# Attention and a SoLU feed-forward on one core: row 0's softmax chain, the scaling of x and the block sums one product later, squares and weight combinations at other places

## The chip, the cores and the metric

The kernel runs on one core of a Trainium2 chip. The metric is the device time of one execution in microseconds (us). Engines are named as in the profile: PE is TensorE's matmul queue (PEld its weight loads), DVE is VectorE, ACT ScalarE, POOL GpSimd, SP the engine whose queue issues most of the DMAs. Each engine works through its own queue in the order in which the kernel was written; between engines there are only waits on semaphores.

## The reference

```python
q_n, k_n = rmsnorm(q, g_q), rmsnorm(k, g_k)              # (8, 12, 448, 64)
scores = q_n @ k_n^T / sqrt(64)
attn = exp(scores - max) / (sum + 1e-9)
x = (attn @ v) with the heads put side by side           # (3584, 768)
h = x @ w_in                                             # (3584, 1024)
sm = exp(h - max) / (sum + 1e-9)
solu = h * sm
ln = (solu - mean) / sqrt(var + 1e-6) * g_ln
out = ln @ w_out                                         # (3584, 768)
```

All of it is float32 in the kernel; the weights arrive as float64 and are converted on the core.

## The kernel before, in words

`fast_path` has three stages, written one after the other in one order for all engines (`manual_schedule`): what stands earlier in the code stands earlier in its engine's queue. `unit(f)` does a piece of TensorE work and then whatever is due; `later(n, f)` makes f due at the end of the n-th unit from there (of the running one for n = 1); `follow(parts, i, f)` puts f right behind part i. Things due at the same unit's end go by their due time and then in the order in which they were entered.

**Attention** (to about 308 us). The 96 heads are worked in 24 quads, m = 0 to 23, two pairs of heads each. A quad m has seven blocks of scores (`score(0)` to `score(6)`, L876), each followed on ACT by an exponential (L836; the last one's output is El), and seven of values (`value`, L888). The sums over keys are made by TensorE from additions of the exponentials (es, L896 and L902 on DVE), for two quads at a time behind every even quad (L948). Beside them, for quads ahead, runs the norm of q and k: `squares` (ACT, L687), `row_sums` (DVE, L693), `fold_sums` (POOL, L703 and L704), `rsqrt_seed` (ACT, a logarithm and an exponential, L710 and L711), `rsqrt_step` (DVE), `normalise` (POOL, L726), `qk_transpose` (DVE, L747) and `gains` (ACT, L742). From quad 6 on (`early`) the squares are made one quad sooner. The conversion of w_in (`convert_w`, quads 5 to 21) and its combinations for the fast product (`combine_in`, POOL, L567) are spread over the quads.

**The w_in products** (about 308 to 568 us). x is worked in 14 groups g of 256 rows, as 2 x 2 blocks with seven products instead of eight (six matmul records each, all on L1097). The order of the parts around group g is

p6(g), p5(g), p7(g), p1(g+1), p4(g), p2(g+1), p3(g).

p6 and p7 add to bank A what p1 left in it, and ACT copies the bank between (L1104: q1 after p1, u2 after p6, u3 after p7). p5 and p3 share bank B, p4 has bank D; both lie in one tile, BD. DVE adds bank and copy into h and takes the running maximum (`plus`, L1113): row 1 of a group is complete after p4, row 0 after p3. Then each row of 128 goes through the chain of `done`: exponential (ACT, L1168), product with h (DVE, L1182), deviations (ACT, L1193), spread (POOL, L1198 to L1201, its last output is `shift`), norm (ACT, L1221), transpose and store (DVE, L1231). In groups 0 to 11 the chain has these six steps (`two_pass`), in the last two groups another form.

Beside it the next group's operand is made: `scale` multiplies x by the inverse sums in three pieces (DVE, L1045; pieces 0 and 1 the two halves of the first 128 rows, piece 2 the other 128 rows), `sizes` takes its squares for a check of range (ACT, L1056, into the tile of the block sums), `block_sums` makes s1 and s2 (POOL, L1073, L1074; they wait for `sizes`), then s3 and s4 (L1076, L1077). p1 needs piece 0, p2 piece 1, p6 needs s2, p5 s1, p7 s3, p3 s4. Behind every third part of groups 0 to 6 a piece of w_out is converted (ACT L538, L539; DVE L545, L546; ACT L551), and 44 combinations of w_out (POOL, L567) stand behind the parts from number 30 on, from part 54 on behind each.

**The w_out products** (from 568 us) follow in the same way with prepared operands.

Of the kernel before, what the change touches and what calls it, by code (L numbers as in the profile page):

```python
# [366 lines left out]
def fast_path(  # L367
# [628 lines left out]
    gs = {}  # L996
# [82 lines left out]
    def products(g, done):  # L1079


        k = {}
        n = DFF // 2

        def mul(bank, a, i, begin=True):
            a11, a12, a21, a22 = gs[g, "A"]
            sm = gs[g, "s"]
            a = {"a11": a11, "a12": a12, "s3": a21, "a22": a22, "s1": sm[:, 0], "s2": sm[:, 1], "s4": sm[:, 2]}[a]
            if begin:
                if bank in "AC" or bank == "B" and g == NG - 1:  # L1090
                    k[bank] = ps_t.tile([P, 512], FP32, tag="t", name=bank, bufs=3)[:, 0:n]
                else:
                    if "BD" not in k:
                        k["BD"] = ps_t.tile([P, 2, 512], FP32, tag="o", name="BD", bufs=1)
                    k[bank] = k["BD"][:, "BD".index(bank), 0:n]
            for c in range(HD):
                nc.tensor.matmul(  # L1097
                    k[bank], a[:, c], w_in[i][:, c],
                    start=begin and c == 0, stop=c == HD - 1, skip_group_check=not begin,
                )  # L1100

        def part(name, bank):
            k[name] = sums_in.tile([P, 512], FP32, tag="part", name=name, bufs=4)[:, 0:n]
            nc.scalar.copy(k[name], k[bank])  # L1104

        def plus(row, col, bank, x):
            t = 2 * g + row
            d = mt.setdefault(t, {})  # L1110
            out = half_of(t, col)
            top = small.tile([P, 1], FP32, tag="top", name="top")
            nc.vector.tensor_tensor_reduce(  # L1113
                out, k[bank], k[x], 1.0, d.get("top", -3.4e38), OP.add, OP.max, top
            )
            d["top"] = top

        def p1():
            mul("A", "a11", 0)
            part("q1", "A")  # L1120

        def p2():
            mul("C", "a12", 1)
            plus(0, 0, "C", "q1")

        def p6():
            mul("A", "s2", 5, False)
            part("u2", "A")

        def p5():  # L1130
            mul("B", "s1", 3)

        def p7():
            mul("A", "s3", 4, False)
            part("u3", "A")
            plus(1, 1, "B", "u3")

        def p4():
            mul("D", "a22", 6)
            plus(1, 0, "D", "u3")  # L1140
            done(1)

        def p3():
            mul("B", "s4", 2, False)
            plus(0, 1, "B", "u2")
            done(0)

        return {1: p1, 2: p2, 3: p3, 4: p4, 5: p5, 6: p6, 7: p7}
# [90 lines left out]
    def in_parts():  # L1239
        def done(g, i):  # L1240
            t = 2 * g + i
            ff_max(t)
            waits = {
                (NG - 2, 1): (1, 2, 3, 5, 5), (NG - 2, 0): (1, 2, 4, 6.25, 7),
                (NG - 1, 1): (1, 2, 3.25, 6.75, 7.25), (NG - 1, 0): (2.25, 4.25, 6.75, 8, 8.75),
            }.get((g, i))
            if two_pass(t):
                steps = (ff_exp, ff_mult, ff_deviations, ff_spread_of, ff_norm, ff_spread)
                waits = (1, 2, 3, 4, 5, 7 if i else 8)
            else:  # L1250
                steps = (ff_exp, ff_mult, ff_moments, ff_norm, ff_spread)
            for x, f in zip(waits, steps):
                later(x, lambda f=f: f(t))

        p = [products(g, lambda i, g=g: done(g, i)) for g in range(NG)]
        parts = [p[0][1], p[0][2]]
        for g in range(NG):
            turn = [p[g][6], p[g][5], p[g][7], p[g][4], p[g][3]]
            x = len(parts)
            if g + 1 < NG:  # L1260
                turn[3:] = [p[g + 1][1], p[g][4], p[g + 1][2], p[g][3]]
            parts += turn
            if g + 1 < NG:
                follow(parts, x, lambda g=g: scale(g + 1, 0))
                follow(parts, x + 1, lambda g=g: scale(g + 1, 1))
                follow(parts, x + 2, lambda g=g: scale(g + 1, 2))
                if g + 2 < NG:
                    follow(parts, x + 3, lambda g=g: load_r(g + 2))
                follow(parts, x + 2, lambda g=g: sizes(g + 1))
                follow(parts, x + 3, lambda g=g: block_sums(g + 1, 0))  # L1270
                follow(parts, x + 4, lambda g=g: block_sums(g + 1, 1))
            if g + 2 < NG:
                follow(parts, x + 4, lambda g=g: load_x(g + 2))
        return parts
# [171 lines left out]
    def follow(p, i, f):  # L1446
        g = p[i]

        def both():
            g()  # L1450
            later(1, f)

        p[i] = both
# [22 lines left out]
    EARLY = 6  # L1476
    steps_at = (5, 6, 8, 9, 11, 12, 14, 15, 17, 18, 20, 21)
    combines_at = {10 + x + 2 * (x // 4): (x,) for x in range(8)}
    combines_at.update({22: (8, 9), 23: (10, 11)})
    inverts_at = {4: (0,), 8: (1,), 10: (2,), 14: (3,), 16: (4,), 20: (5,), 22: (6,)}  # L1480
    wq += [(moe_w_out, c + k, i) for c in range(HF) for k in (0, HF) for i in range(2)]
    again = [(w, w.shape[0] // P, i) for w in (moe_w_in, moe_w_out) for i in range(-(-w.shape[0] // P * w.shape[1] // S))]
# [30 lines left out]
    with tc.manual_schedule():  # L1513
# [68 lines left out]
        for m in range(1, NQ):  # L1582
            a, b = 2 * m, 2 * m + 1
            next1 = m + 1 < NQ
# [4 lines left out]
            def score(x):  # L1589
                unit(lambda: both_scores(m, x))  # L1590
# [50 lines left out]
            else:  # L1641
                if next1:
                    rsqrt_step(norms[m + 1])
                    if m == 2:
                        add_pair(1, 3, 4)
                        quads[1]["terms"].append((2, quads[1]["E", 5]))
                    normalise(a + 2)
                    normalise(b + 2)
                if early:
# [7 lines left out]
                if m == NQ - 1:  # L1657
                    scale(0)
                score(0)
                if m > 3 and not early:  # L1660
                    squares(a + 4)
                    row_sums(a + 4)
                score(1)
                if next1:
                    qk_transpose(a + 2)
                if m > 3 and not early:
                    squares(b + 4)
                    row_sums(b + 4)
                if m <= 3:
                    score(2)  # L1670
                    squares(a + 4)
                    row_sums(a + 4)
                if next1:
                    qk_transpose(b + 2)
                if m > 3:
                    score(2)
                score(3)
                if m <= 3:
                    squares(b + 4)
                    row_sums(b + 4)  # L1680
                if next2:
                    fold_sums(m + 2)
                for x in combines_at.get(m, ()):
# [7 lines left out]
                score(5)  # L1691
                if m in steps_at:
                    low_bits[1]()
                if next1:
                    gains(m + 1)
                add_pair(m, 0, 1)
                add_to(m, 0, 2, nc.vector)
# [4 lines left out]
                    add_pair(m, 3, 4)  # L1702
                value(2)
                score(6)
                if m in steps_at:
                    join()
                if next2:
# [218 lines left out]
```

## Time and profile before

| what | us |
|---|---|
| median of 3 runs (804.02 to 805.27) | 804.84 |
| the profiled execution | 802.92 |
| its span, first to last instruction | 801.1 |
| PE busy | 784.1 |
| DVE busy | 596.2 |
| ACT busy | 502.0 |
| POOL busy | 499.0 |

The mean granted TensorE clock of the profiled execution is 0.998. In the timeline a row has its start and its length in us, the engine (with a q where its queue issues a DMA), the source line, the operation, output<-inputs by the program's names, the shapes and the number of merged instructions; in brackets how long the engine was idle before it and what ended that.

### The profile page before, as it was taken

What the parts mean: (1) busy time and instruction counts of PE and PEld (TensorE: products, weight loads), DVE (VectorE), ACT (ScalarE), POOL (GpSimd) and SP (SyncE); (2) the same over time, 40 slices, a digit from 0 to 9 for tenths busy, and PEclk for the clock granted to TensorE, in tenths of its full rate; (3) what the DMA queues carried; (4) which work ended last, traced back from release to release, by engine and by line L of the source; (5) the groups of instructions that cost most, each with busy time, mean ns of one, the idle gap of its engine ahead of it and who ended that gap; (6) DMA issues with size and microseconds to landing.
All of it is one profiled execution on the core that took longest, in us unless ns stands there. A gap on an engine that the chain in (4) does not pass through costs nothing.

```text
span 801.1 us, 15270 instructions
## 1 busy us (share of the span) xinstructions
PE 784.1 (98%) x5374; PEld 479.2 (60%) x5374; DVE 596.2 (74%) x1061; ACT 502.0 (63%) x822; POOL 499.0 (62%) x618
## 2 busy tenths in 40 slices
PE   8999999999999999999999999999999999999996
PEld 4444444444444444444444444444799999999996
DVE  6877988999899873667776666676896785876854
ACT  6776988788988853677767656554515445464510
POOL 2555453664465461444657589898787777867861
PEclk9999999999999999999999999999999999999999
DMA  9889988888988256566767767673657557357212
GB/s 179 173 167 186 207 196 177 178 201 178 178 193 186 68 152 143 139 171 171 199 162 183 161 151 182 163 177 74 204 151 236 170 178 265 127 197 252 84 61 84
DMA packets 279851, 134.28 MB, mean 168 GB/s; under 512 B 190356, under 2 KB 264916, under 8 KB 279764
## 3 DMA queue, kind: packets, MB, share of 16 engines
q1 hardware_dynamic: 265924, 123.31, 61.7%
q10 hardware_dynamic: 13840, 9.90, 4.6%
q8 instruction: 44, 0.72, 0.4%
q14 instruction: 43, 0.35, 0.1%
HBM read 96.12 MB, written 37.04 MB: 166 GB/s over the span
## 4 chain that ended last, share of the span: by engine, by line
PE 63%; DVE 9%; POOL 8%; DMA 6%; ACT 5%; SPq 4%; issue 4%; DVEq 0%; ACTq 0%; POOLq 0%
PE A L1352 14%; PE s L876 13%; PE o L888 13%; PE B L1352 7%; PE sm L948 4%; PE A L1097 4%; PE BD L1097 4%; PE C L1352 3%; POOL w_out L567 3%; SPq L644 2%; PE C L1097 2%; DMA xg<-xd 1%; DMA raw<-in_moe_w_out_dram 1%; POOL xsum L1077 1%; DVE ub L1231 1%
## 5 line engine op out<-in xcount | busy, mean ns | idle before, releaser
L726 POOL TENSOR_TENSOR qkn<-qk,ny 128x896 f32<-128x896 f32 x45 | 77.2, 1736 | 103.3 <-DVE ny L720 89.3
L876 PE MATMUL s<-qkT 64*64 64x448 f32 x1288 | 139.9, 542 | 0.3 <-ACT qkT L742 0.2
L836 ACT ACTIVATE E<-s 128x896 f32<-128x896 f32 x144 | 124.4, 920 | 18.8 <-PE s L876 18.0
L888 PE MATMUL o<-E,v 64*64 64x448 f32 x1104 | 120.2, 536 | 0.0
L876 PEld LDWEIGHTS s<-qkT 64*64 64x64 f32 x1288 | 65.3, 191 | 60.8 <-issue 41.6
L1352 PE MATMUL A<-w_out,sums 128*128 128x192 f32 x392 | 80.0, 327 | 1.1 <-DVE u L1366 1.1
L1352 PE MATMUL B<-w_out,sums 128*128 128x192 f32 x392 | 79.9, 327 | 0.4 <-DVE P L1414 0.4
L888 PEld LDWEIGHTS o<-E,v 64*64 64x64 f32 x1104 | 42.0, 133 | 56.5 <-issue 49.9
L1097 PE MATMUL A<-w_in,xg 128*128 128x512 f32 x168 | 74.9, 594 | 0.5 <-ACT u L1104 0.5
L1097 PE MATMUL BD<-w_in,xsum 128*128 128x512 f32 x156 | 71.5, 594 | 1.6 <-DVE top L1113 1.5
L1352 PEld LDWEIGHTS A<-w_out,sums 128*128 128x128 f32 x392 | 66.1, 190 | 2.1 <-issue 1.4
L1352 PEld LDWEIGHTS B<-w_out,sums 128*128 128x128 f32 x392 | 66.3, 190 | 1.0 <-DVE P L1414 0.9
L747 DVE STREAM_TRANSPOSE qkT<-qkn 128x896 f32<-128x896 f32 x46 | 50.9, 1106 | 13.6 <-POOL qkn L726 13.5
L1097 PEld LDWEIGHTS A<-w_in,xg 128*128 128x128 f32 x168 | 31.7, 190 | 41.2 <-issue 38.2
L896 DVE TENSOR_TENSOR es<-E 128x896 f32<-128x896 f32 x46 | 55.5, 1206 | 0.5 <-ACT E L836 0.4
L693 DVE TENSOR_REDUCE part<-sq 128x28 f32<-128x896 f32 x46 | 48.0, 1074 | 7.7 <-ACT sq L687 7.7
L1097 PEld LDWEIGHTS BD<-w_in,xsum 128*128 128x128 f32 x156 | 29.3, 190 | 40.2 <-issue 35.8
L567 POOL TENSOR_TENSOR w_out<-w_out 128x384 f32<-128x384 f32 x44 | 50.2, 1142 | 1.7
L1221 ACT ACTIVATE u<-u,shift,he 128x1024 f32<-128x1024 f32 x28 | 34.7, 1239 | 26.2 <-POOL shift L1201 18.0
L1073 POOL TENSOR_TENSOR xsum<-xg 128x384 f32<-128x384 f32 x14 | 14.0, 1000 | 52.1 <-ACT xsum L1056 41.1
L1352 PE MATMUL A<-w_out,s 128*128 128x192 f32 x224 | 45.6, 326 | 0.0
L1182 DVE CUSTOM_DVE_ANT_0 u<-h,u 128x1024 f32<-128x1024 f32 x24 | 36.1, 1503 | 7.7 <-ACT u L1168 7.3
(180 smaller groups left out, 1672.2 us busy)
## 6 DMA issues: line engine op xcount, KB each, us to landing
ur<-ud SPq DMA_DIRECT2D x60, 256.0 KB
ud<-ub SPq DMA_DIRECT2D x112, 128.0 KB
xd<-xo SPq DMA_DIRECT2D x48, 224.0 KB
qk<-in_q_dram SPq DMA_DIRECT2D x92, 112.0 KB
qk<-in_k_dram SPq DMA_DIRECT2D x92, 112.0 KB
v<-in_v_dram SPq DMA_DIRECT2D x23, 448.0 KB
out_dram<-P SPq DMA_DIRECT2D x19, 384.0 KB
raw<-in_moe_w_in_dram SPq DMA_DIRECT2D x12, 512.0 KB
```

The source lines that it names most:

```text
L567: nc.gpsimd.tensor_tensor(o, p, q, OP.subtract)
L693: nc.vector.tensor_reduce(norms[m]["part"][:, i], st[n]["sq"], AX, OP.add)
L726: e.tensor_tensor(d["qkn"].rearrange("p (s b) d -> p s b d", s=2), d["qk"].rearrange("p s (b d) -> p s b d", d=32), y.rearrange("p (s b) - ...
L747: nc.vector.transpose(d["qkT"].rearrange("p s t -> p (s t)"), d["qkn"].rearrange("p b d -> p (b d)"))
L836: nc.scalar.activation(e, s[:, :, 0:S], AF.Exp)
L876: nc.tensor.matmul(s[i * D : (i + 1) * D, h, 0:S], qkT[hh, i, 1, keys], qkT[hh, i, 0], start=True, stop=True)
L888: nc.tensor.matmul(d["o"][h * D : (h + 1) * D, i, 0:S], d["v"][pp, h, kc], d["E", kc][pp, h], start=kc == 0, stop=kc == NK - 1,)
L896: nc.vector.tensor_tensor(e, d["E", x], d["E", y], OP.add)
L1097: nc.tensor.matmul(k[bank], a[:, c], w_in[i][:, c], start=begin and c == 0, stop=c == HD - 1, skip_group_check=not begin,)
L1182: nc.vector.tensor_tensor_reduce(u, h, u, 1.0, 0.0, OP.mult, OP.add, total)
L1221: nc.scalar.activation(d["u"], d["u"], AF.Identity, scale=d["e"], bias=d["shift"])
L1352: nc.tensor.matmul(k[bank], a[:, c].rearrange("p a i -> p (a i)"), w_out[:, area, i, c], start=begin and c == 0, stop=c == KC - 1, skip_gr ...
```

## The change

It touches three things.

- w_in products, row 0 of each two-pass group: every step of its chain but the last comes one unit later. Row 1 is untouched. Scaling: pieces 1 and 2 both come behind part x+2 (p7), not behind x+1 and x+2; `sizes` and both `block_sums` come one part later. Since p1 of a group may now be written before the tile of its block sums exists, `mul` looks that tile up only where a product uses it.
- Attention, quads 2 to 5 in the code's m: for m = 3 the squares and row sums of quad 5 stand behind `score(0)` and `score(1)`, where m = 4 and later have them; for m = 2 both squares come before the second `qk_transpose`; for m = 2 to 5 `gains` stands behind `score(6)` rather than behind `score(5)`.
- Combinations of w_in: numbers 8 and 9 stand ahead of the normalisation in quad 22; 10 and 11 take their former place there, and quad 23 has none.

```diff
         def mul(bank, a, i, begin=True):
             a11, a12, a21, a22 = gs[g, "A"]
-            sm = gs[g, "s"]
-            a = {"a11": a11, "a12": a12, "s3": a21, "a22": a22, "s1": sm[:, 0], "s2": sm[:, 1], "s4": sm[:, 2]}[a]
+            if a in ("s1", "s2", "s4"):
+                a = gs[g, "s"][:, ("s1", "s2", "s4").index(a)]
+            else:
+                a = {"a11": a11, "a12": a12, "s3": a21, "a22": a22}[a]
...
                 steps = (ff_exp, ff_mult, ff_deviations, ff_spread_of, ff_norm, ff_spread)
-                waits = (1, 2, 3, 4, 5, 7 if i else 8)
+                waits = (1, 2, 3, 4, 5, 7) if i else (2, 3, 4, 5, 6, 8)
...
                 follow(parts, x, lambda g=g: scale(g + 1, 0))
-                follow(parts, x + 1, lambda g=g: scale(g + 1, 1))
-                follow(parts, x + 2, lambda g=g: scale(g + 1, 2))
+                follow(parts, x + 2, lambda g=g: (scale(g + 1, 1), scale(g + 1, 2)))
...
-                follow(parts, x + 2, lambda g=g: sizes(g + 1))
-                follow(parts, x + 3, lambda g=g: block_sums(g + 1, 0))
-                follow(parts, x + 4, lambda g=g: block_sums(g + 1, 1))
+                follow(parts, x + 3, lambda g=g: sizes(g + 1))
+                follow(parts, x + 4, lambda g=g: block_sums(g + 1, 0))
+                follow(parts, x + 5, lambda g=g: block_sums(g + 1, 1))
...
-    combines_at.update({22: (8, 9), 23: (10, 11)})
+    combines_first = {22: (8, 9)}
+    combines_at[22] = (10, 11)
...
+                    for x in combines_first.get(m, ()):
+                        combine_in(x)
                     normalise(a + 2)
                     normalise(b + 2)
...
-                if m > 3 and not early:
+                if m > 2 and not early:
                     squares(a + 4)
                     row_sums(a + 4)
                 score(1)
                 if next1:
                     qk_transpose(a + 2)
-                if m > 3 and not early:
+                if m > 2 and not early:
                     squares(b + 4)
                     row_sums(b + 4)
-                if m <= 3:
+                if m == 2:
                     score(2)
                     squares(a + 4)
                     row_sums(a + 4)
-                if next1:
-                    qk_transpose(b + 2)
-                if m > 3:
-                    score(2)
-                score(3)
-                if m <= 3:
+                    score(3)
                     squares(b + 4)
                     row_sums(b + 4)
+                    qk_transpose(b + 2)
+                else:
+                    if next1:
+                        qk_transpose(b + 2)
+                    score(2)
+                    score(3)
...
-                if next1:
+                if next1 and early:
                     gains(m + 1)
...
                 score(6)
+                if next1 and not early:
+                    gains(m + 1)
```

## The prediction

> **What bounds the kernel now.** I read the page's head first, then TensorE's waits between 308 and 568 us (the w_in products; line, releaser, us in all, times, longest).
>
> ```profile
> span 801.1 us, 15270 instructions
> PE 784.1 (98%) x5374; PEld 479.2 (60%) x5374; DVE 596.2 (74%) x1061; ACT 502.0 (63%) x822; POOL 499.0 (62%) x618
> ```
> ```profile
> ...
> PE A L1097 <- ACT u L1104: 0.5, 1, 0.5
> ```
>
> TensorE runs without a break but for short waits, and the change leaves its work alone. So the whole question is how many waits go and how many come. An idle time here is less than what it costs, since TensorE also restarts slowly; I therefore take losses from stretches of time. Next view: stretches from the start of one group of w_in products (or one quad of heads) to the start of the next (start:end, length, then busy time of PE, PEld, DVE, ACT, POOL, clock, DMA).
>
> ```profile
> 331.09:554.85 223.76, 219.50 (x506) 94.65 (x505) 150.74 (x280) 148.78 (x248) 159.03 (x211) 1.00 0.65 162
> 367.60:386.81 19.21, 18.56 (x43) 7.81 (x42) 13.76 (x26) 13.98 (x25) 10.08 (x16) 1.00 0.76 189
> 386.81:406.08 19.27, 18.70 (x44) 7.73 (x43) 15.20 (x28) 15.13 (x26) 13.40 (x17) 1.00 0.77 200
> 406.08:424.91 18.83, 18.29 (x44) 7.89 (x42) 12.57 (x26) 13.22 (x23) 10.24 (x16) 1.00 0.64 163
> 424.91:444.35 19.44, 18.44 (x43) 7.81 (x42) 14.58 (x26) 14.22 (x25) 14.24 (x20) 1.00 0.74 184
> 462.38:480.40 18.02, 18.02 (x43) 7.97 (x42) 11.38 (x24) 10.39 (x17) 15.96 (x21) 1.00 0.56 142
> 480.40:554.85 74.45, 73.17 (x170) 31.59 (x169) 47.72 (x84) 42.58 (x70) 67.32 (x85) 1.00 0.63 154
> 61.62:75.92 14.30, 14.30 (x181) 6.58 (x173) 11.38 (x19) 9.32 (x14) 8.02 (x11) 1.00 0.98 204
> 111.99:125.41 13.42, 13.42 (x172) 6.55 (x165) 12.23 (x20) 11.04 (x15) 5.37 (x7) 1.00 0.79 172
> 160.10:173.90 13.80, 13.80 (x181) 6.76 (x173) 12.93 (x18) 11.42 (x16) 7.53 (x8) 1.00 0.83 181
> 281.12:295.80 14.68, 13.62 (x172) 6.41 (x165) 11.70 (x13) 6.92 (x8) 10.59 (x6) 1.00 0.63 173
> ```
>
> Group 8 (462.38) has no wait: 18.02 us, 2.574 a product. Groups 1 to 12 take 223.76 against 12 x 18.02 = 216.24: **7.52 us are lost**, namely group 3 1.19, group 4 1.25, group 5 0.81, group 6 1.42, groups 9 to 12 together 74.45 - 72.08 = 2.37, and 0.48 in the rest. Quads with the same number of matmuls show quad 4 (61.62) 14.30 - 13.80 = 0.50 late and quad 22 (281.12) 14.68 - 13.42 = 1.26 late. More than about 9.3 us can't be won at these places.
>
> **The w_in products, step by step.** No instruction is added or removed; the order on ACT, DVE and POOL changes. The timeline of group 9 shows why groups 9 to 12 lose:
>
> ```profile
> 485.55 5.31 PE L1097 MATMUL A<-w_in,xg 128*128 128x512 f32 x12
> 487.32 0.19 POOL L1201 TENSOR_TENSOR shift<-um,he 128x1 f32<-128x1 f32 x1
> 487.55 1.24 ACT L1221 ACTIVATE u<-u,shift,he 128x1024 f32<-128x1024 f32 x1 [3.79 <-POOL shift L1201]
> 488.69 1.13 ACT L1193 ACTIVATE h<-u,um 128x1024 f32<-128x1024 f32 x1
> 489.82 0.56 ACT L1104 COPY u<-A 128x512 f32<-128x512 f32 x1
> 490.42 0.69 DVE L1113 CUSTOM_DVE_ANT_0 h<-BD,u 128x512 f32<-128x512 f32 x1 [3.88 <-ACT u L1104]
> 491.17 2.84 PE L1097 MATMUL BD<-w_in,xg 128*128 128x512 f32 x6 [0.31 <-DVE top L1113]
> 492.02 0.84 ACT L1056 ACTIVATE xsum<-xg 128x768 f32<-128x768 f32 x1 [1.64 <-DVE xg L1045]
> 494.00 1.00 POOL L1073 TENSOR_TENSOR xsum<-xg 128x384 f32<-128x384 f32 x1 [1.01 <-ACT xsum L1056]
> 495.08 1.01 POOL L1074 TENSOR_TENSOR xsum<-xsum,xg 128x384 f32<-128x384 f32 x1
> ```
>
> ACT stands still until POOL's shift (487.51), then does the norm of row 1 (L1221), the deviations of row 0 (L1193), and only then the copy u3 (L1104) for which DVE's sum (490.42) and so p4 (491.17) wait. p4 could have begun at 485.55 + 2 x 2.574 = 490.70.
>
> The change delays row 0 by one product, so its deviations come behind u3 in ACT's queue. Then u3 begins at 487.55 + 1.24 = 488.79, 1.03 earlier; by the same distances p4 could go at 491.17 - 1.03 = 490.14, and **the wait is gone with 0.56 to spare**. For groups 9 to 12 I take 2.1 of the 2.37 (bounds: nothing, if POOL's shift comes over 0.6 later than now; 2.37). The second half of group 3's loss is the same wait (p4 again): 0.6. In group 4 TensorE waited for ACT's copy u2 behind row 0's exponential and a weight conversion; that exponential now comes behind u2: 1.0 of 1.25 (bounds 0.5 and 1.25). The conversions that begin after p7 now start on ACT ahead of the size checks, not behind them, which takes the 0.48 and group 4's rest: 0.5 (bounds 0 and 0.73). Together 4.2.
>
> What is late next? Scaling of x's second half moves behind p7's sum on DVE, so the sizes (L1056, two of 0.84) wait for one scaling more. The groups of the stage by line (count, busy, mean ns) have its price and that of a combination of w_out:
>
> ```profile
> L567 POOL TENSOR_TENSOR w_out<-w_out 128x384 f32<-128x384 f32 x44 | 50.2, 1142 | 1.7
> ...
> L1045 DVE TENSOR_TENSOR xg<-xg,rg 128x384 f32<-128x384 f32 (+1 forms) x39 | 28.7, 755 | 5.2 <-DMA ur<-ud 1.9 <-DMA ud<-ub 1.4 <-issue 1.1
> ```
>
> The sizes can begin at 490.42 - 1.03 + 0.75 + 2 x 0.755 = 491.65, against 492.02 now: what the wait held up pays for the second scaling. Where u3 is on time already, as in group 8, they come 0.75 later, and POOL's s1 and s2 (L1073, L1074) with them. p6 of the next group, three products behind p4, at 498.42, needs s2, which ends at 496.09: cover 2.33. One combination more (1.14) now stands ahead of s1 on POOL; it mostly fills the 1.01 that POOL idles there. Behind a late p6 everything on TensorE would wait; that is a rival below.
>
> Two losses stay, by these rows:
>
> ```profile
> 365.35 1.14 ACT L1168 ACTIVATE u<-h,hmax 128x1024 f32<-128x1024 f32 x1
> ...
> 369.84 0.76 DVE L1113 CUSTOM_DVE_ANT_0 h<-BD,u,top 128x512 f32<-128x512 f32 x1
> 370.66 2.84 PE L1097 MATMUL BD<-w_in,xsum 128*128 128x512 f32 x6 [0.32 <-DVE top L1113]
> 414.62 0.64 ACT L538 ACTIVATE tmp<-raw,seven 128x384 f32<-128x384 uint32 x1 [1.88 <-DMA raw<-in_moe_w_out_dram]
> ```
>
> In group 3 (0.6), and in the same way in group 6 (1.3), p5 waits for DVE's sum of p3, queued behind row 1's product and a conversion; row 1's exponential (365.35) is late because ACT's sizes and row 0's norm precede it, and they still do. In group 5 (0.8) u3 stands behind a conversion that waits for its DMA; nothing of that moves. As the ACT work between u3 and row 1's exponential grows by the deviations (1.13), I charge 0.4 for new waits of this kind (bounds 0 and 12 x 0.6 = 7). **w_in: 4.2 - 0.4 = 3.8 saved.**
>
> **Quad 22.** Rows of POOL, DVE and TensorE, with a lone addition (276.25) and the spread of the combinations (minimum/median/maximum):
>
> ```profile
> 295.28 0.58 PE L948 MATMUL sm<-es,ones 128*32 128x224 f32 x8 [1.06 <-DVE es L896]
> 283.46 3.35 POOL L726 TENSOR_TENSOR qkn<-qk,ny 128x896 f32<-128x896 f32 x2 [7.15 <-DVE ny L720]
> 286.77 7.52 POOL L567 TENSOR_TENSOR w_in<-w_in,w_in 128x512 f32<-128x512 f32 x4
> 276.25 1.09 DVE L902 TENSOR_TENSOR es<-es,E 128x896 f32<-128x896 f32 x1
> 289.09 4.05 DVE L902 TENSOR_TENSOR es<-es,E 128x896 f32<-128x896 f32 x2
> 293.07 2.16 DVE L896 TENSOR_TENSOR es<-E 128x896 f32<-128x896 f32 x1
> L567 POOL TENSOR_TENSOR w_in<-w_in,w_in x12: 1266/2196/2212, 144.0 to 292.3; 128x512 f32<-128x512 f32 x12
> ```
>
> Four combinations of w_in run beside DVE's additions, which take 4.05 + 2.16 = 6.21 for three instead of 3 x 1.09 = 3.27: 2.94 more, 0.74 a combination. The last ends at 295.23, and the sums wait 1.06. The change puts two of the four ahead of the normalisation, into POOL's idle 7.15; two of 1.27 to 2.20 fit there, even behind the last conversion. If they ran over, the normalisation (283.46) and with it the next keys' transposes and gains would be late, which TensorE needs only 12 us later. The other two cost 1.47, so the last addition ends at 293.76, 1.47 earlier than now, and the wait of 1.06 with its restart goes: 1.1 of 1.26.
>
> The Trainium skill's page "SBUF — State Buffer", section "Who interferes with whom", speaks against so much: a DVE instruction with two SBUF inputs and a GpSimd one that reads SBUF hold their common port one at a time, and the loser waits for the whole instruction. By that rule two combinations could still hold DVE up by 2 x 1.27 = 2.54, end the additions at 289.09 + 3.27 + 2.54 = 294.90 and leave 0.7 of the wait, so that quad 22 would win 0.3. The trace agrees that they hold each other up (1.09 against 2.0), but at 0.74 a combination.
>
> I keep 1.1, with bounds 0.7 (two cost 2.2, three quarters of what four cost now) and 1.26.
>
> **Quads 2 to 5.** In quads 2 and 3 squares and row sums come earlier, so the fold on POOL and the logarithm on ACT do; quads 2 to 5 do the gains behind the last exponential.
>
> ```profile
> 62.50 0.34 ACT L710 ACTIVATE ny<-ss,eps 128x56 f32<-128x56 f32 x1 [2.04 <-POOL ss L704]
> 86.63 0.98 PE L888 MATMUL o<-El,v 64*64 64x448 f32 x8 [0.54 <-ACT El L836]
> 88.76 1.70 ACT L836 ACTIVATE E<-s 128x896 f32<-128x896 f32 x2
> ```
>
> The logarithm at 62.50 stood 2.04 for POOL's fold and pushed quad 4's first exponential back; squares two scores earlier (2 x 0.75) bring it into ACT's idle time: quad 4's 0.50, less what the squares now cost ahead of quad 3's exponentials (between 0 and the 0.50 that quad 4 shows with that order). At 86.63 the last values wait 0.54 for the exponential (El) that the gains precede; it will be on time, but ACT's queue is as long, quad 6's first exponential stays near 88.76, and its scores wait there instead: 0 (bounds 0 and 0.54). **Together 0.3** (bounds -0.3 and 1.0).
>
> **Sum.** 3.8 + 1.1 + 0.3 = 5.2 us. The profiled execution took 802.92 us (span 801.1), so 797.7; it is 1.92 below the median of the timed runs, 804.84, and against that median I forecast **799.6 us**.
>
> **The rivals.**
> 1. *The ring holds.* From shift to s1 (487.51 to 494.00) and from s1 to the next shift POOL, ACT and DVE wait for each other; POOL is busy 67.32 of 74.45 in groups 9 to 12. If s1's later place delays the next shift by over 0.6, p4 waits as before: of w_in only groups 1, 3 and 4 pay (2.1), less the 0.4: 1.7 + 1.4 = 3.1 won, 801.7. For: POOL has 7.1 to spare in these four groups. Against: the order of its combinations lets it fill the wait.
> 2. *Slower: POOL bounds groups 8 to 12.* Sizes a whole product later (2.57) with a combination (1.14) ahead of s1 make s2 3.7 late against the cover of 2.3: p6 loses 1.4 in each of five groups, 7.0, and the 2.1 of their p4 is not won. 7.0 - 1.7 - 1.4 = 3.9 slower, 808.7. It decides from the point where s2 ends more than 18.0 us after its group began. For: POOL's load. Against: the wait on sizes is on DVE's scaling, which by the sum above isn't later.
> 3. *All waits go*, p5's too, because ACT is freed earlier: 7.5 + 1.3 + 0.3 = 9.1 won, 795.7. Against: rows 365.35 and 414.62.
> 4. *It doesn't do what it says:* the waits only move, or the w_out products, which begin with DVE full, give the gain back: 804.5.
>
> **How the numbers follow.** The forecast has 0.57 (its own range 797.5 to 801.5), rival 1 0.20, rival 2 0.08, rival 3 0.07, rival 4 0.08. A measurement of this kernel tells about 0.2%, 1.6 us, from no change. Faster: 0.57 + 0.16 of rival 1 + 0.07 = 0.80; the same: 0.04 + 0.08 = 0.12; slower: 0.08. The range has to hold rivals 1 and most of 4 and nearly reach 3: 796.5 to 804.0, which leaves out rival 2, part of 3 and tails.
>
> **What would show it.** p4 (L1097, BD from xg) starting without a wait in groups 9 to 12, and group periods at 18.0 to 18.2; ACT's L1193 behind L1104; no POOL wait before L1073 there; two L567 before 283 us and the sums near 294 without a wait; the logarithm of quad 3 near 61 us. p5's waits near 370 and 428 and group 5's should remain. Wrong would be p6 waiting for POOL, p5 waiting in most groups, or periods of 18.6 as before.

## The result and the profile after

The changed kernel takes 799.51 us (median of 5, 798.85 to 801.64) against 804.84: ratio 0.9939, 95% interval 0.9923 to 0.9954, so 5 us or 0.6% faster. The forecast was 799.6. The profiled execution of it took 799.23 us, 3.7 less than that of before; up to the w_out products it is 4.0 ahead, and these take 0.3 longer.

First the page's head. The engines' counts are those of before; DVE is busy 6.6 us less:

```profile
span 797.4 us, 15261 instructions
PE 781.3 (98%) x5374; PEld 480.4 (60%) x5374; DVE 589.6 (74%) x1061; ACT 503.4 (63%) x822; POOL 496.9 (62%) x618
```

The stretches that answer to those of the prediction (start:end, length, busy time of PE, PEld, DVE, ACT, POOL, clock, DMA): groups 1 to 12, group 9, 10, 11, 12, group 3, then quads 4 and 22.

```profile
329.08:550.85 221.77, 217.88 (x506) 95.25 (x504) 146.31 (x282) 149.41 (x248) 159.65 (x211) 1.00 0.68 164
477.26:495.28 18.02, 18.02 (x43) 7.98 (x42) 10.52 (x21) 11.58 (x20) 16.65 (x22) 1.00 0.71 167
495.28:513.31 18.03, 18.03 (x44) 7.98 (x43) 11.94 (x22) 10.67 (x18) 16.75 (x21) 1.00 0.70 171
513.31:532.82 19.51, 18.55 (x43) 7.81 (x42) 11.95 (x22) 10.62 (x18) 15.18 (x22) 1.00 0.67 170
532.82:550.85 18.03, 18.03 (x44) 7.98 (x42) 10.77 (x19) 10.54 (x17) 17.15 (x21) 1.00 0.51 116
366.06:385.32 19.26, 18.29 (x43) 7.89 (x42) 15.56 (x29) 14.06 (x24) 9.31 (x15) 1.00 0.79 197
61.22:75.13 13.91, 13.91 (x181) 6.68 (x173) 11.37 (x18) 8.96 (x12) 7.31 (x8) 1.00 1.00 204
280.37:293.79 13.42, 13.42 (x173) 6.56 (x165) 10.43 (x14) 6.92 (x8) 7.87 (x5) 1.00 0.73 190
```

Groups 9, 10 and 12 run without a wait, as group 8 did before. Group 11 loses 1.5 us and group 2 0.9, which is new. Group 3 loses as much as before, though now all at p5. Quad 22 is at the 13.42 of an undisturbed quad; quad 4 won 0.4. Groups 1 to 12 won 2.0 us (223.76 to 221.77) where I had said 3.8; the stretch ahead of them won 2.0 as well (group 0 begins at 311.06, before at 313.07; 0.2 of it lies ahead of the first changed quad), where I had said 1.4.

The timeline of group 10 shows the wait of p4 gone by the way described: row 0's deviations (L1195, before L1193) now follow the copy u3 (L1106), and POOL's s1 starts (508.25) just behind the sizes, without an idle time.

```profile
503.21 0.59 ACT L1106 COPY u<-A 128x512 f32<-128x512 f32 x1 [1.70 <-PE A L1099]
503.69 1.15 ACT L1195 ACTIVATE h<-u,um 128x1024 f32<-128x1024 f32 x1
...
507.23 0.84 ACT L1056 ACTIVATE xsum<-xg 128x768 f32<-128x768 f32 x1
508.25 1.28 POOL L1073 TENSOR_TENSOR xsum<-xg 128x384 f32<-128x384 f32 x1
```

Group 11 shows what is late in its place. ACT issues the next x at 509.62; DVE's scaling of it (L1045) stands idle 4.81 us for a load and begins at 520.53; p1 waits for the scaling (521.65). p4 waits (524.99) for DVE's sum (524.25), which stands behind the late scaling and two more DVE instructions: an addition for the w_out products (L1314, 521.53) and, in its new place, row 0's product with h (1.21 us from 522.92).

```profile
509.62 1.12 ACTq L1009 DMA_DIRECT2D xg<-xd  x2
520.53 1.06 DVE L1045 TENSOR_TENSOR xg<-xg,rg 128x384 f32<-128x384 f32 x1 [4.81 <-DMA ur<-ud]
521.53 1.47 DVE L1314 TENSOR_TENSOR s<-ur 128x512 f32<-128x512 f32 x1
521.65 2.84 PE L1099 MATMUL A<-w_in,xg 128*128 128x512 f32 x6 [0.46 <-DVE xg L1045]
524.25 0.68 DVE L1115 CUSTOM_DVE_ANT_0 h<-BD,u 128x512 f32<-128x512 f32 x1
524.99 2.84 PE L1099 MATMUL BD<-w_in,xg 128*128 128x512 f32 x6 [0.50 <-DVE top L1115]
```

The load named there (ur) is only the one that landed last; what the scaling reads is x and rg, which were under way at the same time, and the trace doesn't tell which of the two it waited for.

### The profile page after: what moved, and what is told of

It is laid out like the page before. It is cut to its first block, busy times and chain, and to the rows that moved or that the text cites. A ratio compares the mean times of both kernels' runs of the same rounds, so it can differ in the third digit from the quotient of the medians.

```text
span 797.4 us, 15261 instructions
## 1 busy us (share of the span) xinstructions
PE 781.3 (98%) x5374; PEld 480.4 (60%) x5374; DVE 589.6 (74%) x1061; ACT 503.4 (63%) x822; POOL 496.9 (62%) x618
## 4 chain that ended last, share of the span: by engine, by line
PE 80%; DVE 6%; DMA 6%; ACT 3%; SPq 2%; issue 1%; POOL 1%; DVEq 0%; ACTq 0%; POOLq 0%
PE A L1353 14%; PE s L876 14%; PE o L888 14%; PE A L1099 9%; PE BD L1099 8%; PE B L1353 7%; PE sm L948 4%; PE C L1353 3%; PE C L1099 3%; DMA xg<-xd 2%; DMA raw<-in_moe_w_out_dram 2%; DMA ur<-ud 2%; PE pt L790 1%; DVE ub L1233 1%; ACT E L836 1%
## 5 line engine op out<-in xcount | busy, mean ns | idle before, releaser
L836 ACT ACTIVATE E<-s 128x896 f32<-128x896 f32 x144 | 124.5, 921 | 20.1 <-PE s L876 19.3
L567 POOL TENSOR_TENSOR w_out<-w_out 128x384 f32<-128x384 f32 x44 | 45.4, 1034 | 1.1
L1045 DVE TENSOR_TENSOR xg<-xg,rg 128x384 f32<-128x384 f32 (+1 forms) x39 | 28.5, 759 | 22.5 <-DMA ud<-ub 7.0
L1195 ACT ACTIVATE h<-u,um 128x1024 f32<-128x1024 f32 x24 | 27.6, 1150 | 22.0 <-DVE um L1185 22.0
```

Of the source, the lines that this page charges most:

```text
L567: nc.gpsimd.tensor_tensor(o, p, q, OP.subtract)
L836: nc.scalar.activation(e, s[:, :, 0:S], AF.Exp)
```

## The experiments

Times are medians, each beside a before measured on the same chip. The last column is the trace's length from the start of group 1 to that of group 13 (12 x 18.02 = 216.2 without any wait).

| kernel | us | before | ratio (95%) | groups 1 to 12 |
|---|---|---|---|---|
| whole_again | 800.53 | 805.5 | 0.9939 (0.9925 to 0.9952) | 222.74 |
| in_only | 802.68 | 805.5 | 0.9968 (0.9957 to 0.9978) | 222.65 |
| combos_only | 804.59 | 805.5 | 0.9987 (0.9977 to 0.9997) | 226.58 |
| quads_only | 804.62 | 805.5 | 0.9988 (0.9979 to 0.9997) | 225.07 |
| row0_only | 803.78 | 805.31 | 0.9988 (0.9978 to 0.9997) | 224.70 |
| moves_only | 806.70 | 805.31 | 1.0019 (1.0009 to 1.0029) | 228.03 |
| ur_later | 797.69 | 805.31 | 0.9910 (0.9894 to 0.9925) | 220.08 |
| conv_later | 799.77 | 805.31 | 0.9934 (0.9921 to 0.9947) | 222.69 |
| before_ur | 804.50 | 805.23 | 0.9989 (0.9979 to 0.9999) | 225.21 |
| ur_load | 801.57 | 805.23 | 0.9955 (0.9941 to 0.9969) | 223.66 |
| ur_load_conv | 802.02 | 805.23 | 0.9960 (0.9947 to 0.9973) | 223.00 |
| ur_x | 797.24 | 804.86 | 0.9905 (0.9888 to 0.9921) | 219.07 |

**The parts by themselves.** Each is the kernel before with one part of the change's diff.

> The kernel before with the edits of the w_in products alone (row 0 one unit later, scaling, sizes and block sums moved); attention as before. Theory (the parts of the sum are independent, and w_in pays as forecast): 3.8 us faster, near 801.0. In the profiled execution of the changed kernel groups 1 to 12 took 221.77 us against 223.76, so only 2.0 less; if that holds on every execution, 802.8. Rival (the w_in part pays nothing of itself, the waits only move from one group to another): within 1 us of 804.8. In the trace all three differ in groups 9 to 12: 72.1 to 72.4 us together by the theory, over 74 by the rival.

> The kernel before with the combinations of w_in alone moved (8 and 9 ahead of quad 22's normalisation, 10 and 11 in their place, none in quad 23). Theory: the wait of the sums near 295 us goes, quad 22 takes 13.4 us instead of 14.68, and the whole is 1.1 to 1.3 us faster, 803.6. Rival (two combinations hold the additions up as long as they run themselves, 2.5 us): quad 22 takes 14.4, 804.5. Second rival: the gain in quad 22 is real but is lost at the start of the w_in products, where the first scaled x or a load is awaited: quad 22 at 13.4 and the whole within 0.4 of before.

> The kernel before with the edits of quads 2 to 5 alone (squares and row sums earlier, gains behind the last exponential). Theory, from the profiled execution of the changed kernel: quad 4 gains 0.4, quads 5 and 6 change by -0.8 and +0.8, together 0.3 to 0.6 us faster, 804.3. Rival (the squares cost ahead of the exponentials what they gain behind): no difference, 804.8, or 0.3 slower.

> The changed kernel itself a second time, for a second profile. Theory (the waits that remain are set by the order of the work): near 799.5, and the same five waits as in its first profile: p4 of group 2 (0.93), p5 of groups 3 and 6 (1.2 and 0.8), p7 and p1 of group 4 (1.0), p1 and p4 of group 11 (1.5). Rival (those behind late loads, in groups 2, 4 and 11, are chances of one execution): p5's waits in groups 3 and 6 return, the others appear elsewhere or not at all.

From the ratios: w_in 2.6 us (interval 1.8 to 3.5), quad 22 1.05 (0.2 to 1.9), quads 2 to 5 0.97 (0.2 to 1.7); their sum 4.6 against 4.9 for the whole. The parts add up. In the traces the attention parts return to a few hundredths: quad 22 is 13.42 in combos_only and 14.68 to 14.72 where its edit is missing, and from quad 2 to the end of quad 6 the time is 64.55 to 64.58 us with the edit, 65.12 to 65.16 without.

The w_in stage doesn't return so well. With the old order four profiles give 223.76, 226.58, 225.07 and 225.21 for groups 1 to 12 (the last is before_ur, below, which differs in one pair of loads), with the new one three give 221.77, 222.74 and 222.65. So the profile that I worked from was the best of four, and the gain between the means is 225.16 - 222.39 = 2.8, in agreement with in_only. By place:

| mean of the profiles | groups 1 to 8 | groups 9 to 12 |
|---|---|---|
| old order (4) | 150.4 | 74.75 |
| new order (3) | 148.3 | 74.1 |
| without any wait | 144.2 | 72.1 |

whole_again decides for its theory in the main: p5's waits in groups 3 and 6 (1.23 both), p1's and p4's in group 11 (1.5) and the loss in group 4 are there again, group 2's is 0.29 instead of 0.93, and in group 12 p1 and p4 lose another 1.0. So the waits behind loads are no chance of one execution, though their sizes are.

**The two halves of the w_in edit.**

```diff
 row0_only:
-                waits = (1, 2, 3, 4, 5, 7 if i else 8)
+                waits = (1, 2, 3, 4, 5, 7) if i else (2, 3, 4, 5, 6, 8)
 moves_only:
+                follow(parts, x + 2, lambda g=g: (scale(g + 1, 1), scale(g + 1, 2)))
...
+                follow(parts, x + 3, lambda g=g: sizes(g + 1))
+                follow(parts, x + 4, lambda g=g: block_sums(g + 1, 0))
+                follow(parts, x + 5, lambda g=g: block_sums(g + 1, 1))
```

> The kernel before with row 0's chain one unit later and nothing else. Theory (p4's waits come from row 0's deviations ahead of u3 on ACT, and this edit alone puts them behind): in groups 9 to 12 the losses at p4 (before: 0.57, 0.89, 0.26 and 0.60) are gone, and the whole gains most of what all w_in edits gain together (2.8 in the timed runs), 803.3 to 802.7. Rival (the steps only pay together: without the later sizes, row 0's deviations now stand beside the sizes and hold up q or s2): within 1 us of before, with p4 clean and new losses at p2 or p6.

> The kernel before with scaling, sizes and block sums moved and row 0's chain left where it was. Theory (u3 still stands behind row 0's deviations): p4's losses in groups 9 to 12 stay at 2.0 to 2.8 together, and the gain is at most that of group 1's p3 and of the start of the w_in conversions (0.4 to 0.8), 804.7 to 805.2 beside a before of 805.5. Rival (the place of the sizes frees the ring of POOL, ACT and DVE): p4's losses there under 1.0 and a gain of over 1.5.

row0_only, stretches of group 9 and 11:

```profile
481.13:499.16 18.03, 18.03 (x43) 7.98 (x42) 11.86 (x24) 11.63 (x20) 16.01 (x21) 1.00 0.74 170
...
517.18:537.48 20.30, 18.56 (x43) 7.81 (x42) 11.92 (x20) 10.65 (x17) 15.00 (x22) 1.00 0.67 163
```

Row 0's delay alone clears p4 in groups 9, 10 and 12, and alone brings up the wait of group 11 (p1 0.9, p4 1.3). So row 0's deviations ahead of u3 were what held p4, as the prediction had it. Its gain is only 1.0 us (0.2 to 1.8), between the theory's 2.0 and the rival's nothing. Group 4 gives the rest back: it loses 3.0, against 1.2 to 2.0 in the four profiles of the old order. p7 and p1 lose 1.8 of it (before 1.0) and p3 1.2 (before 0.3), where a conversion begun behind the sizes puts its two DVE instructions ahead of the sum of p4.

The moves alone make the kernel 1.5 us slower (0.7 to 2.3), which neither theory had. p4's losses in groups 9 to 12 fall to 1.0 in all (and group 8 loses 0.5, which it didn't before), so the later sizes help there too; but groups 3, 5 and 6 lose 1.9, 1.5 and 2.0 at p4, group 4 1.7 at p7, and group 11 2.0 at p1. ACT's rows in group 5 show why there: the norm of row 1 waits for POOL's shift, and behind it stand row 0's deviations, a conversion, and only then u3 (418.24).

```profile
414.87 1.24 ACT L1223 ACTIVATE u<-u,shift,he 128x1024 f32<-128x1024 f32 x1 [1.49 <-POOL shift L1203]
416.02 1.13 ACT L1195 ACTIVATE h<-u,um 128x1024 f32<-128x1024 f32 x1
...
417.15 0.62 ACT L538 ACTIVATE tmp<-raw,seven 128x384 f32<-128x384 uint32 x1
...
418.24 0.57 ACT L1106 COPY u<-A 128x512 f32<-128x512 f32 x1
```

So 2.6 for both is 1.0 and -1.5 for the halves: they need each other. Why POOL's shift is as late as it is with the moves alone was not taken apart.

**The wait in group 11.** ur_later is the changed kernel with

```diff
-        follow(parts, 77, lambda: early("s1", 3, (0, 1)))
+        follow(parts, 79, lambda: early("s1", 3, (0, 1)))
```

and before_ur is the kernel before with the same line. `early` enters the two loads of ur and makes the DVE addition that uses them (L1314) due three parts later, so both move.

> The changed kernel with one pair of loads for the w_out products (ur, entered at part 77, in group 10) entered two parts later. In the changed kernel p1 waits in group 11 for the scaling of x, which waits for a load (0.62 in two profiles, 1.68 with the w_in edits alone), and p4 waits 0.87 behind it. Theory (with p4's wait in group 10 gone, the next x has no time left to land beside the ur loads): both waits of group 11 go, group 11 takes 18.0 to 18.2 us instead of 19.52, and the whole is 1.0 to 1.5 us faster than the changed kernel, near 798.8. Rival (x itself needs that long, whatever else is loaded): group 11 still at 19.5. Second rival: the collision only moves to the next x, and group 12 loses the same.

> The kernel before with the ur loads of group 10 entered two parts later, as in ur_later, and nothing of the change. Theory (the wait for x in group 11 is one that the change laid bare: before, p4's wait in group 10, 0.9, gave x's load its time): nothing to win, within 0.5 us of before, and p4's losses in groups 9 to 12 as before (2.3 together). Rival (those loads cost time with any order): 1.5 to 2 us faster, as with the change.

```profile
512.61:531.20 18.59, 18.46 (x43) 7.82 (x42) 12.73 (x21) 10.62 (x17) 15.01 (x20) 1.00 0.62 160
```

Group 11 of ur_later falls from 19.51 to 18.59 (p1 0.3 and p4 0.3 remain, of 0.6 and 0.9), group 12 has no wait, and groups 1 to 12 take 220.08, less than in any profile of the changed kernel. Its median is 797.69. In the old order the same edit wins nothing there: groups 9 to 12 take 74.64 us (74.45 to 75.13 without it), p4 of group 10 still loses 0.9. Its timed 0.9 us (0.1 to 1.7) is more than I had said, hardly apart from nothing, and doesn't come from these groups.

So ur_later tries two things at once. p1's gain can't come from the addition, which stands behind the scaling in the changed kernel too. p4's can: the addition now runs at 525.74, behind p4's sum, and that sum begins 10.02 into the group instead of 10.94. How much of p4's gain is the loads' and how much the addition's stays open.

The theory holds in half. Worked out from the timelines (ACT's issue of the x for group 12, the start and length of the first scaling, p1):

| kernel | issue to scaling | first scaling | p1 waits |
|---|---|---|---|
| before, combos_only, quads_only | 10.7, 11.0, 10.5 | 0.56 each | 0 |
| before_ur | 10.2 | 0.56 | 0 |
| changed, whole_again, in_only | 10.9, 10.6, 12.2 | 1.06, 1.29, 0.90 | 0.6, 0.6, 1.7 |
| conv_later (below) | 11.0 | 0.77 | 0.8 |
| ur_later | 10.8 | 0.90 | 0.3 |
| ur_load, ur_load_conv (below) | 10.4, 9.6 | 1.33, 0.56 | 0.6, 0 |
| ur_x (below) | 10.3 | 1.42 | 0 |

With the ur loads out of the way (before_ur, ur_later, ur_load, ur_load_conv, ur_x) x and rg still take 9.6 to 10.8 us, 10.3 in the mean, so the first rival has its share; with them it is 10.5 to 12.2 in the seven other profiles of this table. And the scaling, 0.56 in every profile of the old order, is longer in every one of the new but one: POOL's combinations now run beside it. In the one, ur_load_conv, it begins at 521.83, a combination ends at 521.84 and the next begins at 523.73, and it takes 0.56 again. The account for the first profiles: p1 begins three products (7.73) into group 11. Before, x was issued 15.02 into a group 10 of 18.93, which leaves 18.93 - 15.02 + 7.73 = 11.64 for 10.69 + 0.56: 0.39 to spare. Now it is issued 14.34 into a group of 18.02, which leaves 11.41 for 10.92 + 1.06: 0.57 short. Of that turn of 0.96 the shorter group makes 0.23, the load 0.23 and the scaling 0.50. (My expectation had put all of group 10's 0.9 into it; but x is issued behind p4 and moves with it.)

**p5's wait in groups 3 and 6.**

```diff
-            follow(parts, 3 * (x - n_in) + 2, lambda x=x: convert_next(x))
+            i = x - n_in
+            follow(parts, 3 * i + 2 + (i % 7 == 6), lambda x=x: convert_next(x))
```

> The changed kernel with two of the conversions of w_out (those that begin behind p4 of groups 2 and 5) begun one part later, so that their two DVE instructions stand behind DVE's sum of p3 and not ahead of it. Theory (p5's waits in groups 3 and 6, 1.2 and 0.8 to 1.2, come from that order on DVE alone): both groups take 18.0 to 18.2, and the whole is 1.8 to 2.3 us faster than the changed kernel, near 798.0. Rival (row 1's late exponential holds DVE's product, and with it p3's sum, up anyway, as my prediction had it): half of the waits stays. Second rival: the conversion now stands ahead of the copy u3 or u2 on ACT, and p7 or p4 loses what p5 wins.

The changed kernel in group 3, where DVE's sum of p3 (368.97) stands behind the conversion's two instructions, which run beside POOL's s3 and s4 (L1076, L1077):

```profile
366.36 1.00 POOL L1076 TENSOR_TENSOR xg<-xg 128x384 f32<-128x384 f32 x1
...
366.40 1.38 DVE L545 SCALAR_TENSOR_TENSOR tmp<-raw,tmp 128x384 uint32<-128x384 uint32 x1
...
367.32 1.31 POOL L1077 TENSOR_TENSOR xsum<-xg,xsum 128x384 f32<-128x384 f32 x1
...
367.81 1.23 DVE L546 SCALAR_TENSOR_TENSOR tmp<-raw,tmp 128x384 uint32<-128x384 uint32 x1
...
368.97 0.74 DVE L1115 CUSTOM_DVE_ANT_0 h<-BD,u,top 128x512 f32<-128x512 f32 x1
...
369.77 0.70 PE L1099 MATMUL BD<-w_in,xsum 128*128 128x512 f32 x1 [0.97 <-DVE top L1115]
```

conv_later at the same place, and then where it loses again:

```profile
366.29 0.75 DVE L1115 CUSTOM_DVE_ANT_0 h<-BD,u,top 128x512 f32<-128x512 f32 x1
...
368.44 0.52 DVE L545 SCALAR_TENSOR_TENSOR tmp<-raw,tmp 128x384 uint32<-128x384 uint32 x1
...
373.42 0.65 ACT L538 ACTIVATE tmp<-raw,seven 128x384 f32<-128x384 uint32 x1 [2.09 <-DMA raw<-in_moe_w_out_dram]
...
375.66 0.56 ACT L1106 COPY u<-A 128x512 f32<-128x512 f32 x1
```

p5's waits are gone in both groups, so of the two things that I had ahead of DVE's sum, row 1's product behind its late exponential and the conversion, it was the conversion. But p4 now loses 0.72 and 1.05 there: the next conversion, whose raw was loaded the later for it, holds ACT for 2.09 us ahead of u3. No gain of the size expected (0.9934 against 0.9939); the second rival holds.

**Loading raw sooner.** ur_load is ur_later with `later(2, load_next)` for `later(3, load_next)`; ur_load_conv has conv_later's edit as well.

> ur_later with the loads of raw w_out (load_next behind a conversion) entered one part sooner, ahead of a store or of rg in SP's queue. Theory (in groups 2 and 4 a conversion stands on ACT ahead of a copy u and waits for its raw, which is late because its load stands behind others in SP's queue): p7's and p1's losses in group 4 (0.6 and 0.75 in ur_later, up to 2.0 elsewhere) and p4's in group 2 (0.3 to 0.9) go, 1.0 to 1.8 us faster than ur_later, 796.0 to 796.7. Rival (the sixteen DMA engines are full there, sooner issued isn't sooner landed): no gain. Second rival: rg behind it comes later, and p1 waits for the scaling instead.

> ur_load with the two conversions of conv_later begun one part later as well. Theory (in conv_later p4 lost in groups 3 and 6 what p5 won because the shifted conversions' successors waited for their raw ahead of u3; with the raws sooner they don't): both groups at 18.0 to 18.3, 1.5 to 2.0 us faster than ur_load. Rival (the conversions' own length on ACT ahead of u3 is enough to hold p4): groups 3 and 6 at 18.7 to 19.1 as in conv_later, within 0.7 of ur_load.

Groups 4 and 5 of ur_load:

```profile
385.49:403.55 18.06, 18.06 (x43) 7.89 (x42) 12.49 (x28) 14.66 (x25) 11.43 (x18) 1.00 0.76 196
403.55:424.00 20.45, 18.42 (x43) 7.81 (x42) 12.66 (x23) 13.78 (x23) 12.58 (x18) 1.00 0.61 149
```

Group 4 is rid of its waits as the theory said (19.38 in ur_later), and groups 3, 5 and 6 lose more than that, 1.2, 2.4 and 1.0 over ur_later, above all at p1, which waits for the scaling of x (2.8 us in three waits, one of them in group 11): 3.6 us slower than ur_later by the ratios. That is the second rival, at a higher price than I had given it. ur_load_conv shows the same (groups 3, 5 and 6 at 20.8, 20.1 and 19.9), which neither its theory nor its rival had. In these groups the loads stand in each other's way: with raw issued sooner, x comes later.

**x sooner.** ur_x is ur_later with ACT's issue of the next x ahead of row 0's norm: `load_x` becomes due a quarter of a unit earlier.

> ur_later with ACT's issue of the next x ahead of row 0's norm and not behind it, so 1.2 us (one L1223) sooner. Theory (group 11's last 0.57 is p1 waiting for x, and in group 4 p1's 0.75 too): group 11 at 18.0, group 4 under 19.0, the whole 0.5 to 1.3 us faster than ur_later, near 797.0. Rival (the loads of groups 2 to 6 compete, as ur_load showed: x sooner makes raw later, and the conversion's wait ahead of u grows): group 11 gains its 0.5, groups 2 to 6 lose as much, no difference that can be measured.

Groups 9 to 12 now run without any wait (x is issued 13.07 into group 10, and the scaling ends 0.9 before p1 needs it); group 3 takes 18.45 instead of 19.17, group 4 19.65 instead of 19.38. The scaling begins 1.7 us earlier in group 11 than in ur_later though rg is issued later (0.5 to 1.1 us), which speaks for x as the load that held it. But one profile doesn't show it: in ur_load_conv, with x issued 14.54 into group 10, groups 9 to 12 have no wait either. In time ur_x can't be told from ur_later (0.9905 and 0.9910). Both are faster than the kernel before by 7 us, and by some 2 us than the change; the interval of ur_later ends where that of whole_again begins, and they were not timed side by side.

## Why the prediction was right, and where not

The time came out at the forecast, with the sum 5.2 against 4.9 to 5.3 measured, and the parts by their measured sizes: w_in 2.6 to 2.8 (forecast 3.8, bounds far wider), quad 22 1.05 timed and 1.26 in the trace (1.1), quads 2 to 5 0.97 timed and 0.54 in the trace (0.3). That the total came within 0.1 us is luck: w_in was put 1.0 to 1.2 too high, the traces have the other two terms 0.2 higher each than forecast, and the 0.7 between their sum in the traces, 4.6, and the 5.3 between the medians lies within the interval of the measurement (1.2 us each way).

- **p4 in groups 9 to 12**: the mechanism is right and shown by row0_only; the size is not. Of 2.1 only 0.7 stays between the means. The step that failed is "What is late next?": I followed POOL's s2 and the sizes, and neither the load of x nor the scaling in front of p1. The row that would have told it stands in the profile of before, group 11:

```profile
524.72 0.56 DVE L1045 TENSOR_TENSOR xg<-xg,rg 128x384 f32<-128x384 f32 x1 [1.85 <-DMA ur<-ud]
```

  DVE waits for a load there and is done at 525.28; p1 wanted it at 517.93 + 7.73 = 525.66. A wait on an idle engine, 0.38 ahead of the path, and I cut the groups before it short. Rival 4 says that waits may move, but with the whole gain lost; none of the rivals names this wait.
- **s2 and p6**: right. In groups 9 to 12 POOL stands idle ahead of L1073 for 0.15 us at most (once), no p6 waits for it in any group, and rival 2 fell.
- **p4 in group 3**: gone, as said. **p7 in group 4**: wrong. It loses 1.0 and, with p1, 1.2 and 2.1 in the other two profiles, since the conversion ahead of u2 waits for its raw; taking the exponential away only bares that wait. ACT in group 4 of the changed kernel (u2 follows at 390.69):

```profile
389.59 0.64 ACT L538 ACTIVATE tmp<-raw,seven 128x384 f32<-128x384 uint32 x1 [2.73 <-DMA raw<-in_moe_w_out_dram]
```

  **p3 in groups 1 and 4**: gone, as said. Groups 1 to 8 together win 2.1 between the means, where I had 1.7: p4's loss in group 5, which I had left standing, went too, and part came back in group 2.
- **p5 near 370 and 428**: the waits stay, as said, but of the causes given only the conversion holds: conv_later clears them without touching row 1's exponential.
- **Quad 22**: right to 0.2, but the price was misread. Two combinations cost the additions 0.98 in all (4.25 for three against 3.27), and I had taken 1.47, 0.74 for each. DVE, POOL and TensorE in the changed kernel, each instruction by itself from 286.02 on:

```profile
279.07 2.63 POOL L567 TENSOR_TENSOR w_in<-w_in,w_in 128x512 f32<-128x512 f32 x2 [3.50 <-DVE w_in L546]
...
286.02 1.28 POOL L567 TENSOR_TENSOR w_in<-w_in,w_in 128x512 f32<-128x512 f32 x1
287.14 1.11 DVE L896 TENSOR_TENSOR es<-E 128x896 f32<-128x896 f32 x1
287.38 2.00 POOL L567 TENSOR_TENSOR w_in<-w_in,w_in 128x512 f32<-128x512 f32 x1
288.35 1.98 DVE L902 TENSOR_TENSOR es<-es,E 128x896 f32<-128x896 f32 x1
290.44 1.09 DVE L902 TENSOR_TENSOR es<-es,E 128x896 f32<-128x896 f32 x1
291.44 1.08 DVE L896 TENSOR_TENSOR es<-E 128x896 f32<-128x896 f32 x1
292.92 0.94 PE L948 MATMUL sm<-es,ones 128*32 128x224 f32 x16
```

  The first combination (286.02) runs beside a transpose and costs nothing. The second begins while an addition runs (287.14) and takes 2.00 instead of 1.27; the addition that begins at 288.35 takes 1.98 instead of 1.09 and ends 0.95 after that combination (289.38); the two behind it run alone. In the profile of before it is the same three times over:

```profile
288.12 2.00 POOL L567 TENSOR_TENSOR w_in<-w_in,w_in 128x512 f32<-128x512 f32 x1
289.09 1.98 DVE L902 TENSOR_TENSOR es<-es,E 128x896 f32<-128x896 f32 x1
```

  So the 2.94 there is three waits of about 1 us, not four shares of 0.74. The rule of the Trainium skill ("SBUF — State Buffer", "Who interferes with whom") that I set against my price fits these rows one by one. What left 0.7 of the wait in the estimate by it was my count: I let both combinations hold the additions up for their whole 1.27, and only one met any, already under way.
- **Quads 2 to 5**: quad 4 wins 0.40 and quad 3 loses 0.11, as said, with quad 3's logarithm at 60.21; quad 2 wins 0.28, which I had left out; quads 5 and 6 change by -0.77 and +0.80, since the wait moves from the last values to the next scores, as said:

```profile
88.95 1.04 PE L876 MATMUL s<-qkT 64*64 64x448 f32 x8 [0.54 <-ACT E L836]
```

- **The basis**: losses came from one profile, whose w_in stage was the shortest of four by 1.3. The mean of the four loses 8.9 in groups 1 to 12, and not 7.5, and single groups differ by up to 0.9 from one of these profiles to the next, so a sum of short waits from one profile is no better than that.

## What to carry to other kernels

When a wait is taken away, the work behind it comes sooner, and what it needs from elsewhere may not: for each load on its way read the time between the end of its first use and the instruction that needs that use, also where the idle engine costs nothing now. Where loads crowd a stretch, as in groups 2 to 6 here, issuing one sooner can make another's user wait and lose in all (ur_load). Work that nobody needs yet, a load and what is done with it, is worth moving out of a stretch once the path there hangs on a load: ur_later gained by it in the new order, before_ur next to nothing in the old. And a part of a reordering tried alone can lose where the whole wins (moves_only), so what belongs to one queue's order is tried together.

## What the runs showed of the hardware

**The load of x** (768 KB, with rg beside it) takes 9.6 to 12.2 us from issue to use in group 11 in all fourteen profiles. The DMA share of the sixteen engines (the column before the last) in the changed kernel shows that they are full in the last microseconds before the scaling begins at 520.53:

```profile
515.00:517.00 2.00, 2.00 (x6) 0.95 (x5) 0.72 (x1) 0.92 (x2) 2.00 (x3) 1.00 1.11 263
...
519.00:521.00 2.00, 2.00 (x6) 0.65 (x4) 0.47 (x1) 0.75 (x1) 1.74 (x4) 1.00 0.95 276
```

**DVE beside POOL.** The conversion's two DVE instructions, with two inputs each, take 1.38 and 1.23 us beside POOL's s3 and s4 and 0.52 and 0.56 clear of them: 1.5 more, which covers the 1.24 that group 3 loses at p5. The rule of the Trainium skill named above fits here as in quad 22: each is longer by less than one POOL instruction (1.00 and 1.31), and each ends 0.4 behind the POOL instruction that began ahead of it. The reordering also moved such pairs, apart in one place (the product with h and POOL's combinations) and together in another (the scaling in group 11, 0.56 to 1.06). Groups of the w_in stage before and after (count, busy, mean ns, idle ahead and its cause):

```profile
L1182 DVE CUSTOM_DVE_ANT_0 u<-h,u 128x1024 f32<-128x1024 f32 x23 | 34.9, 1516 | 7.7 <-ACT u L1168 7.3
...
L1221 ACT ACTIVATE u<-u,shift,he 128x1024 f32<-128x1024 f32 x24 | 29.7, 1238 | 18.0 <-POOL shift L1201 18.0
```
```profile
L567 POOL TENSOR_TENSOR w_out<-w_out 128x384 f32<-128x384 f32 x44 | 45.4, 1034 | 1.1
...
L1184 DVE CUSTOM_DVE_ANT_0 u<-h,u 128x1024 f32<-128x1024 f32 x24 | 30.5, 1270 | 2.9 <-ACT u L1170 2.9
L1223 ACT ACTIVATE u<-u,shift,he 128x1024 f32<-128x1024 f32 x24 | 29.5, 1230 | 4.9 <-POOL shift L1203 4.9
```

DVE's product falls from 1516 to 1270 ns, a combination on POOL from 1142 to 1034, and ACT's idle time for POOL's shift from 18.0 to 4.9 us. With row 0's delay alone (row0_only) the product takes 1419 ns in the mean and ACT's idle time is 6.8 us; with the moves alone 1496 ns and 19.6 us. So the idle time goes with row 0's place, and the product needs both. That product and combination get shorter because those pairs were moved apart is argued from the rows, not tried by itself.

**A wait costs more than its length.** p5's wait of 0.97 in group 3 makes the group 1.24 longer (19.26 against 18.02). In a running stream a product starts 0.17 before the one ahead of it has ended (2.74 long, 2.57 apart), which is lost when TensorE has to wait, and the product that waited takes 2.84 instead of 2.74.
